# Attention steps of successive chunks put in one group on the TensorE, and value products as column-tiled pairs, in a fused retention and feed-forward kernel

## The chip, the cores and the metric

The kernel runs on one core of a Trainium2 chip. The metric is the device time of an execution in microseconds (us). Executions of a kernel agree within some tenths of a per cent in most cases, with a few one per cent higher; this case is about one to two per cent, so the comparisons below use several rounds on the same chip and, where possible, the trace. A verdict of the timing (faster, same, slower) is drawn at 2%.

## The reference

```python
# q, k, v: [8 batches, 8 heads, 576 tokens, 64]
scores = q @ k.T / sqrt(64)
ret    = scores * gamma[h] ** (i - j)      # for j <= i, else 0
attn   = ret @ v                           # [8, 8, 576, 64]
x      = attn, heads side by side          # [4608 tokens, 512]
h      = x @ w_in                          # [4608, 2048]
g      = h * sigmoid(beta * h)
out    = g @ w_out                         # [4608, 512]
```

## The kernel before

Each batch is cut into chunks of 128, 128, 128, 128 and 64 tokens ("short chunk"), 40 chunks in all. The decay is separable, so it is put into q and v, and what the earlier chunks of a batch contribute is held in a 64x64 state per head. PE is TensorE, ACT is ScalarE, DVE is VectorE and POOL is GpSimd. A row tile is a part of PE's array that takes 64 of its 128 rows, a column tile one that takes 64 of its 128 columns; in the traces here two matmuls on two such tiles start 3 to 4 ns apart. How the array is divided, whole or in tiles, is called the tiling mode here. A chunk has these steps:

- `pre` (POOL): scale and cast q, k and v;
- `a_T` (PE): transpose q and k; ACT copies the result;
- `a_sc` (PE): scores of the chunk with itself, contraction over 64, so head pairs run as row tiles; DVE applies the causal mask, giving R;
- `a_st` (PE): add k^T v to the state in PSUM; ACT copies its diagonal blocks to `sbd`;
- `a_O` (PE): the output product O = state product (`sbd` times q) plus value product (v times R); DVE casts it to `xT`.

The value product is the part that the change is about. Two heads share the 128 output partitions. Before, each head's 64 value columns lay in a 128-column buffer whose other half was zero, so a full-width matmul added zeros to the other head:

```python
vpads = [consts.tile([P, H, P], BF16, name=f"vpad{i}") for i in range(NV)]   # cleared once
...
def a_O(i):
    ...
    n = 0
    if c > 0:
        for p in range(HP):                                   # state product
            nc.tensor.matmul(O[:, p, :cL], sbds[(i - 1) % NS][:, p, :], L["qT"][:, p, :cL],
                             start=(n == 0), stop=False, skip_group_check=True)
            n += 1
    for j in range(2):
        for p in range(HP):                                   # value product, padded
            nc.tensor.matmul(O[:, p, :cL], vp[:cL, 2 * p + j, :], R[:cL, j, p, :cL],
                             start=(n == 0), stop=(j == 1), skip_group_check=True)
            n += 1
    nc.vector.tensor_copy(xT[:, :, n0:n0 + cL], O[:, :, :cL])
```

The feed-forward part runs over blocks of 512 tokens: 16 calls of `up` (4 matmuls of 512 columns each) and 16 of `down` (4 each). The steps of the chunks that the next block needs are strewn among these calls, in three places per chunk (`at` is a place in the list of calls, `F` puts off a call until its place is reached):

```python
def attn_steps(i, at, gap=2.0):
    return [(at - 4, F(pre, i)), (at - 3.9, F(load_next, i)), (at, F(a_T, i)), (at + gap, F(a_sc, i)),
            (at + 2 * gap, F(a_st, i)), (at + 2 * gap, F(a_O, i))]
```

Of the kernel before, what the change touches and what calls it, by code (L numbers as in the profile page):

```python
# [12 lines left out]
BF16 = mybir.dt.bfloat16  # L13
ACT = mybir.ActivationFunctionType
ALU = mybir.AluOpType
# [4 lines left out]
def kernel(  # L20
# [10 lines left out]
    nc = tc.nc  # L31
    B, H, S, D = q.shape
# [3 lines left out]
    P = 128  # L36
    HP = H // 2
    KO = d_model // P
    FO = d_ff // P
    MB = 512  # L40
    NMB = N // MB
# [4 lines left out]
    consts = ctx.enter_context(tc.tile_pool(name="consts", bufs=1))  # L46
# [3 lines left out]
    sb = ctx.enter_context(tc.tile_pool(name="sb", bufs=2))  # L50
# [16 lines left out]
    order = [(b, c) for b in range(B) for c in range(NC)]  # L67
# [15 lines left out]
    for h in range(H):  # L83
# [11 lines left out]
    nc.gpsimd.affine_select(out=causal[:], in_=causal[:], pattern=[[1, P]], compare_op=ALU.is_ge,  # L95
                            fill=0.0, base=0, channel_multiplier=-1)

    NV = 3
    vpads = [consts.tile([P, H, P], BF16, name=f"vpad{i}") for i in range(NV)]

    NS = 2
    sbds = [consts.tile([P, HP, P], BF16, name=f"sbd{i}") for i in range(NS)]
    nc.gpsimd.memset(vpads[0][:], 0.0)
    nc.vector.memset(sbds[0][:], 0.0)
    nc.gpsimd.memset(vpads[1][:], 0.0)
    nc.vector.memset(sbds[1][:], 0.0)


# [57 lines left out]
    live = {}  # L166

    def pre(i):

        b, c = order[i]  # L170
        c0, cL = chunks[c]
        t = qkv_tiles.pop((b, c))
        first = i < 4
        qn = sb.tile([P, H, D], BF16, name="qn", tag="qn", bufs=3)
        kn = sb.tile([P, H, D], BF16, name="kn", tag="kn", bufs=3)
        vp = vpads[i % NV]

        vp4 = vp.rearrange("p (pr two) (x d) -> p pr (two x) d", two=2, x=2)[:, :, 0::3, :]
        gq_b = gq[:cL, c, :].unsqueeze(2).to_broadcast([cL, H, D])
        gv_b = gv[:cL, c, :].unsqueeze(2).to_broadcast([cL, H, D])  # L180
        (nc.vector if first else nc.gpsimd).tensor_tensor(qn[:cL], t[:cL, 0], gq_b, ALU.mult)  # L181
        if first:
            nc.scalar.copy(kn[:cL], t[:cL, 1])
        else:
            nc.gpsimd.tensor_copy(kn[:cL], t[:cL, 1])  # L185
        nc.gpsimd.tensor_tensor(vp4[:cL], t[:cL, 2].rearrange("p (pr two) d -> p pr two d", two=2),  # L186
                                gv_b.rearrange("p (pr two) d -> p pr two d", two=2), ALU.mult)
        live[i] = dict(qn=qn, kn=kn, vp=vp, vp4=vp4)

    def load_next(i):  # L190
        if i + NQ < len(order):
# [2 lines left out]
    def a_T(i):  # L194
        b, c = order[i]
        c0, cL = chunks[c]
        L = live[i]
        T = psum.tile([P, 2, HP, P], BF16, name="T", tag="T", bufs=1)
        for j, src in enumerate((L["qn"], L["kn"])):
            for p in range(HP):  # L200
                nc.tensor.transpose(T[:, j, p, :cL],  # L201
                                    src[:cL, 2 * p:2 * p + 2, :].rearrange("p h d -> p (h d)"),
                                    ident[:cL, :cL])
        qkT = sb.tile([P, 2, HP, P], BF16, name="qkT", tag="qkT", bufs=3)
        nc.scalar.copy(qkT[:, :, :, :cL], T[:, :, :, :cL])  # L205
        L["qT"], L["kT"] = qkT[:, 0], qkT[:, 1]

# [16 lines left out]
    def a_O(i):  # L224
        b, c = order[i]
        c0, cL = chunks[c]
        L = live[i]
        R, vp = L["R"], L["vp"]
        O = psum.tile([P, HP, P], F32, name="O", tag="O", bufs=1)
        n = 0  # L230
        if c > 0:
            for p in range(HP):
                nc.tensor.matmul(O[:, p, :cL], sbds[(i - 1) % NS][:, p, :], L["qT"][:, p, :cL],  # L233
                                 start=(n == 0), stop=False, skip_group_check=True)
                n += 1
        for j in range(2):
            for p in range(HP):
                nc.tensor.matmul(O[:, p, :cL], vp[:cL, 2 * p + j, :], R[:cL, j, p, :cL],  # L238
                                 start=(n == 0), stop=(j == 1), skip_group_check=True)
                n += 1  # L240
        n0 = b * S + c0
        nc.vector.tensor_copy(xT[:, :, n0:n0 + cL], O[:, :, :cL])  # L242
        del live[i]

    def a_st(i):
        b, c = order[i]
        c0, cL = chunks[c]
        L = live[i]
        if c == NC - 1:
            return  # L250
        if c == 0:
            state_ps[b] = psum.tile([P, HP, P], F32, name="st", tag="st", bufs=1)
        st = state_ps[b]
        for p in range(HP):
            nc.tensor.matmul(st[:, p, :], L["kn"][:cL, 2 * p:2 * p + 2, :].rearrange("p h d -> p (h d)"),  # L255
                             L["vp4"][:cL, p], start=(c == 0 and p == 0), stop=True,
                             skip_group_check=True)
        sbd = sbds[i % NS]
        for j in range(2):
            r = slice(j * D, (j + 1) * D)  # L260
            nc.scalar.copy(sbd[r, :, j * D:(j + 1) * D], st[r, :, j * D:(j + 1) * D])  # L261
# [34 lines left out]
    def merged(fill, *streams):  # L296

        todo = sorted((x for st in streams for x in st), key=lambda x: x[0])
        for n, f in enumerate(fill):
            while todo and todo[0][0] <= n:  # L300
                todo.pop(0)[1]()
            f()
        for _, step in todo:
            step()

    def F(f, *a):
        return lambda: f(*a)
# [6 lines that stand above are left out]
    warm_up(12)  # L314
    betas()
    pre(0)
    a_T(0)
    nc.gpsimd.memset(vpads[2][:], 0.0)
    pre(1)
    for i in range(4):  # L320
        warm_up(2)
        a_sc(i)
        a_st(i)
        if i < 3:
            a_T(i + 1)
            if i < 2:
                pre(i + 2)
        else:
            cast_w_in(0)
            warm_up(2)  # L330
        a_O(i)

    fill = [F(up, 0, fo) for fo in range(FO)]
    merged(fill, [(2, F(cast_w_in, 1)), (5, F(cast_w_in, 2)), (9, F(cast_w_in, 3))],
           [(5.1 + g / 10, F(load_w_out, g)) for g in range(2)],
           [(9.1 + g / 10, F(load_w_out, g)) for g in range(2, WG)],
           [(9.5, F(pre, 4)), (12, F(a_T, 4)), (14, F(a_sc, 4)), (16, F(a_O, 4))],
           [(9.6, F(pre, 5)), (15, F(a_T, 5)), (16.1, F(a_sc, 5))], [(9.7, F(pre, 6))])
    for i in range(5):
        load_next(i)  # L340

    q1 = S + chunks[0][1] - MB
    a_st(5)
    a_O(5)
    load_next(5)
    load_next(6)
    fill = [F(up, 1, fo, 0, q1) for fo in range(FO)]
    fill += [F(down, 0, ms, f0) for f0 in range(0, FO, 4) for ms in range(3)]
    fill += [F(down, 0, 3, f0) for f0 in range(0, FO, 4)]
    n1 = len(fill)  # L350
    fill += [F(up, 1, fo, q1, MB - q1) for fo in range(FO)]
    fill += [F(down, 1, ms, f0) for ms in range(MB // P) for f0 in range(0, FO, 4)]
    streams = [[(4, F(cast_w_out, 0)), (10, F(cast_w_out, 1)), (18, F(cast_w_out, 2)), (21, F(cast_w_out, 3))],
               [(0, F(a_T, 6)), (4, F(a_sc, 6)), (8, F(a_st, 6)), (8, F(a_O, 6))],
               attn_steps(7, 23), attn_steps(8, 27)]
    done = 9
    need = lambda m: min(len(order), next((i + 1 for i, (b, c) in enumerate(order)
                                          if b * S + chunks[c][0] + chunks[c][1] >= (m + 1) * MB), len(order)))
    todo = list(range(done, need(2)))
    streams += [attn_steps(i, n1 + n * 30 / len(todo)) for n, i in enumerate(todo)]  # L360
    done = need(2)
    for m in range(2, NMB):
        base = len(fill)
        fill += [F(up, m, fo) for fo in range(FO)]
        fill += [F(down, m, ms, f0) for ms in range(MB // P) for f0 in range(0, FO, 4)]
        if m + 1 < NMB:
            todo = list(range(done, need(m + 1)))
            streams += [attn_steps(i, base + n * 31 / len(todo)) for n, i in enumerate(todo)]
            done = need(m + 1)
    merged(fill, *streams)  # L370


# [28 lines left out]
```

## Time and profile before

| | before |
|---|---|
| time, median | 338.75 us (338.43 to 338.87, 3 runs) |
| span of the profiled execution | 337.1 us |
| PE busy | 325.6 us, 97% |
| ACT, DVE, POOL busy | 48%, 34%, 34% |
| a block of 512 tokens, start to start | 35.86 and 34.08 us, in turn |
| the projections of the last block, which has no attention, by starts | 27.63 us |

These are the busy times and the chain of work that ended last, from the page of the kernel before (PEld is PE's loading of weights, SPq and POOLq are sequencers that issue work, "issue" is time in which nothing is seen to be waited for).

```profile
PE 325.6 (97%) x2455; PEld 174.0 (52%) x2455; DVE 114.0 (34%) x202; ACT 163.1 (48%) x272; POOL 115.0 (34%) x132
PE 84%; DMA 7%; SPq 4%; issue 1%; DVE 1%; ACT 1%; POOL 0%; POOLq 0%
```

PE is nearly always busy and the chain runs on it. That alone does not say how much a cheaper PE step saves, since the ends of matmuls are modelled. The starts are what to read. The next lines are the PE timeline of the kernel before over one full chunk (start in us, duration in us, engine, line, operation, tile rows and columns, moving operand, count).

```profile
193.43 0.39 PE L201 MATMUL T<-ident,qn 128*128 128x128 bf16 x4
193.65 0.39 PE L201 MATMUL T<-ident,kn 128*128 128x128 bf16 x4
193.87 1.89 PE L285 MATMUL po<-w_out_sb,gT 128*128 128x512 bf16 x8
195.70 0.40 PE L217 MATMUL sc<-qkT 64*128 64x128 bf16 x8
196.03 1.90 PE L285 MATMUL po<-w_out_sb,gT 128*128 128x512 bf16 x8
197.76 0.39 PE L255 MATMUL st<-vpad,kn 128*128 128x128 bf16 x4
197.99 0.39 PE L233 MATMUL O<-qkT,sbd 128*128 128x128 bf16 x4
198.21 0.61 PE L238 MATMUL O<-R,vpad 128*128 128x128 bf16 x8
198.66 0.60 PE L285 MATMUL po<-w_out_sb,gT 128*128 128x512 bf16 x2
```

Differences of starts give the price of each step. The value product (L238) takes 198.66 - 198.21 = 0.45 us: 8 matmuls of 128 columns, 56 ns each. State and state product take 0.22 us each. Eight matmuls of 512 columns take 8 x 0.216 = 1.73 us, yet from 193.87 to the scores at 195.70 there are 1.83 us: 0.10 us are lost as the PE goes from whole-array matmuls (128\*128) to row tiles (64\*128). On the way back the loss repeats: the eight scores run as four pairs, 56 ns apart, 0.22 us in all, but the next projection starts 0.33 us after the scores began. It then goes on 12 ns late. So a change of tiling mode costs about 0.105 us, and about half of the scores' 0.44 us is changes. Transposes, state, state product and value product fit between projections without a gap.

The cost of a full chunk is thus 0.45 + 0.44 + 0.22 + 0.22 + 0.45 = 1.78 us. By the counts in the trace the longer of the two kinds of block runs the steps of five chunks, four full ones and a short one, as a batch has them; the shorter kind has one full chunk less, and 35.86 - 34.08 = 1.78 us again. So the five chunks of a batch cost 35.86 - 27.63 = 8.23 us, 1.65 us for an average chunk. The lengths of their steps in the trace add up to the same 8.23.

### The profile page before, as it was taken

What the parts mean: (1) busy time and instruction counts of PE and PEld (TensorE: products, weight loads), DVE (VectorE), ACT (ScalarE), POOL (GpSimd) and SP (SyncE); (2) the same over time, 40 slices, a digit from 0 to 9 for tenths busy, and PEclk for the clock granted to TensorE, in tenths of its full rate; (3) what the DMA queues carried; (4) which work ended last, traced back from release to release, by engine and by line L of the source; (5) the groups of instructions that cost most, each with busy time, mean ns of one, the idle gap of its engine ahead of it and who ended that gap; (6) DMA issues with size and microseconds to landing.
All of it is one profiled execution on the core that took longest, in us unless ns stands there. A gap on an engine that the chain in (4) does not pass through costs nothing.

```text
span 337.1 us, 6009 instructions
## 1 busy us (share of the span) xinstructions
PE 325.6 (97%) x2455; PEld 174.0 (52%) x2455; DVE 114.0 (34%) x202; ACT 163.1 (48%) x272; POOL 115.0 (34%) x132
## 2 busy tenths in 40 slices
PE   5979899999999999999999999999999999999995
PEld 2644574676554555545555555545555555544442
DVE  4664373623321244213332432223224432320011
ACT  2767671385246623752376227712782257404800
POOL 5224767875324433323334432233333330000000
PEclk9799999999999999999999999999999999999999
DMA  9999999999999737906492549036400100011011
GB/s 173 222 387 212 243 377 214 199 212 229 234 222 246 146 111 172 172 0 158 116 228 48 117 118 214 9 87 159 114 2 31 61 36 0 14 55 57 2 61 63
DMA packets 121979, 46.53 MB, mean 138 GB/s; under 512 B 113232, under 2 KB 113248, under 8 KB 121952
## 3 DMA queue, kind: packets, MB, share of 16 engines
q1 hardware_dynamic: 121920, 46.15, 61.3%
q8 instruction: 19, 0.31, 0.4%
q14 instruction: 8, 0.07, 0.1%
q10 hardware_dynamic: 32, 0.01, 0.0%
HBM read 36.71 MB, written 9.44 MB: 137 GB/s over the span
## 4 chain that ended last, share of the span: by engine, by line
PE 84%; DMA 7%; SPq 4%; issue 1%; DVE 1%; ACT 1%; POOL 0%; POOLq 0%
PE po L285 38%; PE ph L273 32%; DMA qkvn<-in_q_dram 4%; PE O L238 4%; PE T L201 4%; SPq L63 4%; PE sc L217 3%; DMA wt<-in_moe_w_out_dram 2%; PE st L255 2%; PE O L233 2%; SPq L122 1%; ACT gT L275 1%; DVE w_out_sb L141 0%; DVE R L221 0%; ACT qkT L205 0%
## 5 line engine op out<-in xcount | busy, mean ns | idle before, releaser
L273 PE MATMUL ph<-xT,w_in_sb 128*128 128x512 bf16 (+2 forms) x640 | 134.2, 358 | 1.7 <-DVE xT L242 1.7
L285 PE MATMUL po<-w_out_sb,gT 128*128 128x512 bf16 x576 | 133.6, 380 | 0.0
L275 ACT ACTIVATE gT<-ph,beta_sb 128x512 bf16<-128x512 f32 (+2 forms) x160 | 102.0, 645 | 41.2 <-PE ph L273 39.9
L273 PEld LDWEIGHTS <-w_in_sb 128*128 128x128 bf16 x640 | 58.4, 98 | 55.5 <-issue 1.6
L285 PEld LDWEIGHTS <-gT 128*128 128x128 bf16 x576 | 53.3, 98 | 57.9
L221 DVE TENSOR_TENSOR R<-sc,causal 128x512 bf16<-128x512 f32 (+1 forms) x80 | 47.2, 631 | 101.1 <-PE sc L217 101.0
L205 ACT COPY qkT<-T 128x1024 bf16<-128x1024 bf16 (+1 forms) x40 | 36.9, 924 | 68.6 <-PE T L201 68.5
L181 POOL TENSOR_TENSOR qn<-qkvn,gq 128x512 bf16<-128x512 f32 (+1 forms) x36 | 37.9, 1052 | 49.9 <-PE T L201 46.4
L186 POOL TENSOR_TENSOR vpad<-qkvn,gv 128x512 bf16<-128x512 f32 (+1 forms) x40 | 41.6, 1041 | 28.2 <-PE O L238 14.9
L291 DVE COPY ot<-po 128x512 f32<-128x512 f32 x36 | 24.8, 691 | 67.5 <-PE po L285 65.1
L185 POOL CAST kn<-qkvn 128x512 bf16<-128x512 f32 (+1 forms) x36 | 21.9, 608 | 69.5 <-issue 65.7
L261 ACT CAST sbd<-st 64x256 bf16<-64x256 f32 x64 | 23.3, 364 | 43.4 <-PE st L255 42.6
L242 DVE CAST xT<-O 128x512 bf16<-128x512 f32 (+1 forms) x40 | 25.5, 637 | 38.0 <-PE O L238 38.0
L238 PE MATMUL O<-R,vpad 128*128 128x128 bf16 (+1 forms) x320 | 23.7, 214 | 1.4 <-DVE R L221 1.2
L238 PEld LDWEIGHTS <-vpad 128*128 128x128 bf16 (+1 forms) x320 | 18.2, 97 | 2.8 <-issue 2.2
L217 PEld LDWEIGHTS <-qkT 64*128 64x128 bf16 (+1 forms) x320 | 8.9, 98 | 17.3 <-ACT qkT L205 7.1
L201 PE MATMUL T<-ident,qn 128*128 128x128 bf16 (+1 forms) x160 | 15.1, 218 | 2.5 <-DVE qn L181 2.4
L201 PEld LDWEIGHTS <-qn 128*128 128x128 bf16 (+1 forms) x160 | 11.1, 99 | 11.9 <-DVE qn L181 2.4
L217 PE MATMUL sc<-qkT 64*128 64x128 bf16 (+1 forms) x320 | 15.5, 217 | 0.6 <-ACT qkT L205 0.4
L201 PE MATMUL T<-ident,kn 128*128 128x128 bf16 (+1 forms) x160 | 14.9, 216 | 0.3 <-POOL kn L185 0.3
L255 PEld LDWEIGHTS <-kn 128*128 128x128 bf16 x128 | 9.5, 99 | 6.6 <-issue 0.2
L255 PE MATMUL st<-vpad,kn 128*128 128x128 bf16 x128 | 12.7, 222 | 0.0
(40 smaller groups left out, 80.0 us busy)
## 6 DMA issues: line engine op xcount, KB each, us to landing
out_dram<-ot SPq DMA_DIRECT2D x36, 256.0 KB, 2.2
qkvn<-in_q_dram SPq DMA_DIRECT2D x32, 256.0 KB, 4.8
qkvn<-in_k_dram SPq DMA_DIRECT2D x32, 256.0 KB, 5.1
qkvn<-in_v_dram SPq DMA_DIRECT2D x32, 256.0 KB, 5.0
wt<-in_moe_w_in_dram SPq DMA_DIRECT2D x4, 1024.0 KB, 10.6
wt<-in_moe_w_out_dram SPq DMA_DIRECT2D x4, 1024.0 KB, 10.2
qkvn<-in_q_dram SPq DMA_DIRECT2D x8, 128.0 KB, 4.0
qkvn<-in_k_dram SPq DMA_DIRECT2D x8, 128.0 KB, 3.6
```

Of the source, the lines that this page charges most:

```text
L181: (nc.vector if first else nc.gpsimd).tensor_tensor(qn[:cL], t[:cL, 0], gq_b, ALU.mult)
L186: nc.gpsimd.tensor_tensor(vp4[:cL], t[:cL, 2].rearrange("p (pr two) d -> p pr two d", two=2), gv_b.rearrange("p (pr two) d -> p pr two d", ...
L201: nc.tensor.transpose(T[:, j, p, :cL], src[:cL, 2 * p:2 * p + 2, :].rearrange("p h d -> p (h d)"), ident[:cL, :cL])
L205: nc.scalar.copy(qkT[:, :, :, :cL], T[:, :, :, :cL])
L217: nc.tensor.matmul(sc[j][:cL, p, :cL], L["kT"][r, p, :cL], L["qT"][r, p, :cL], start=True, stop=True, skip_group_check=True)
L221: nc.vector.tensor_tensor(R[:cL, j, :, :cL], sc[j][:cL, :, :cL], m_b, ALU.mult)
L238: nc.tensor.matmul(O[:, p, :cL], vp[:cL, 2 * p + j, :], R[:cL, j, p, :cL], start=(n == 0), stop=(j == 1), skip_group_check=True)
L242: nc.vector.tensor_copy(xT[:, :, n0:n0 + cL], O[:, :, :cL])
L255: nc.tensor.matmul(st[:, p, :], L["kn"][:cL, 2 * p:2 * p + 2, :].rearrange("p h d -> p (h d)"), L["vp4"][:cL, p], start=(c == 0 and p == 0 ...
L273: nc.tensor.matmul(ph[:, :tn], w_in_sb[:, ko, fo * P:(fo + 1) * P], xT[:, ko, x0:x0 + tn], start=(ko == 0), stop=(ko == KO - 1))
L275: nc.scalar.activation(gT[:, fo, t0:t0 + tn], ph[:, :tn], ACT.Silu, scale=beta_sb[:, fo:fo + 1])
L285: nc.tensor.matmul(po[:], gT[:, fo, ms * P:(ms + 1) * P], w_out_sb[:, fo, :], start=(fo == 0), stop=(fo == FO - 1))
```

## The change

Its intent is to halve the value product: the two heads of a pair become two column tiles of 64 columns that run at once, without padding. As this gives the value product a tiling mode of its own, the steps of three successive chunks (transposes of chunk i, scores of i-1, output and state of i-2) are put into one group, so that the modes follow on one another. From chunk 9 on there is one group per chunk; chunks 0 to 8 keep their places. The diff, cut to its core:

```diff
-        vp = vpads[i % NV]
-        nc.gpsimd.tensor_tensor(vp4[:cL], ...)                 # strided, into padded buffers
+        vn = sb.tile([P, H, D], BF16, name="vn", tag="vn", bufs=4)
+        nc.gpsimd.tensor_tensor(vn[:cL], t[:cL, 2], gv_b, ALU.mult)
...
         O = psum.tile([P, HP, P], F32, name="O", tag="O", bufs=1)
+        for p in range(HP):
+            for j in range(2):
+                nc.tensor.matmul(O[j * D:(j + 1) * D, p, :cL], vn[:cL, 2 * p + j, :], R[:cL, j, p, :cL],
+                                 start=(p == 0), stop=(c == 0), skip_group_check=True)
         if c > 0:
             for p in range(HP):
                 nc.tensor.matmul(O[:, p, :cL], sbds[(i - 1) % NS][:, p, :], L["qT"][:, p, :cL],
-                                 start=(n == 0), stop=False, skip_group_check=True)
-                n += 1
-        for j in range(2):
-            for p in range(HP):
-                nc.tensor.matmul(O[:, p, :cL], vp[:cL, 2 * p + j, :], R[:cL, j, p, :cL], ...)
+                                 start=False, stop=True, skip_group_check=True)
...
+    def cluster(i, at):
+        last = len(order) - 1
+        st = []
+        if i <= last:
+            st += [(at - 4, F(pre, i)), (at - 3.9, F(load_next, i)), (at, F(a_T, i))]
+        if C0 <= i - 1 <= last:
+            st += [(at, F(a_sc, i - 1))]
+        if C0 <= i - 2 <= last:
+            st += [(at, F(a_O, i - 2)), (at, F(a_st, i - 2))]
+        return st
...
+        todo = list(range(done, need(m + 1) + 2))
+        streams += [cluster(i, base + n * 31 / len(todo)) for n, i in enumerate(todo)]
```

Left out: one more buffer each for k and for the transposed q and k, the state's matmuls, which now read `vn`, and the clearing of the padded buffers, which falls away.

More of the change, by code (lines that the diff above doesn't have):

```diff
@@ L96 @@
                             fill=0.0, base=0, channel_multiplier=-1)
-    NV = 3
-    vpads = [consts.tile([P, H, P], BF16, name=f"vpad{i}") for i in range(NV)]
     NS = 2
     sbds = [consts.tile([P, HP, P], BF16, name=f"sbd{i}") for i in range(NS)]
-    nc.gpsimd.memset(vpads[0][:], 0.0)
     nc.vector.memset(sbds[0][:], 0.0)
-    nc.gpsimd.memset(vpads[1][:], 0.0)
     nc.vector.memset(sbds[1][:], 0.0)
@@ L174, in pre @@
         qn = sb.tile([P, H, D], BF16, name="qn", tag="qn", bufs=3)
-        kn = sb.tile([P, H, D], BF16, name="kn", tag="kn", bufs=3)
-        vp = vpads[i % NV]
-        vp4 = vp.rearrange("p (pr two) (x d) -> p pr (two x) d", two=2, x=2)[:, :, 0::3, :]
+        kn = sb.tile([P, H, D], BF16, name="kn", tag="kn", bufs=4)
+        vn = sb.tile([P, H, D], BF16, name="vn", tag="vn", bufs=4)
         gq_b = gq[:cL, c, :].unsqueeze(2).to_broadcast([cL, H, D])
@@ L185, in pre @@
             nc.gpsimd.tensor_copy(kn[:cL], t[:cL, 1])
-        nc.gpsimd.tensor_tensor(vp4[:cL], t[:cL, 2].rearrange("p (pr two) d -> p pr two d", two=2),
-                                gv_b.rearrange("p (pr two) d -> p pr two d", two=2), ALU.mult)
-        live[i] = dict(qn=qn, kn=kn, vp=vp, vp4=vp4)
+        nc.gpsimd.tensor_tensor(vn[:cL], t[:cL, 2], gv_b, ALU.mult)
+        live[i] = dict(qn=qn, kn=kn, vn=vn)
     def load_next(i):
@@ L203, in a_T @@
                                     ident[:cL, :cL])
-        qkT = sb.tile([P, 2, HP, P], BF16, name="qkT", tag="qkT", bufs=3)
+        qkT = sb.tile([P, 2, HP, P], BF16, name="qkT", tag="qkT", bufs=4)
         nc.scalar.copy(qkT[:, :, :, :cL], T[:, :, :, :cL])
@@ L227, in a_O @@
         L = live[i]
-        R, vp = L["R"], L["vp"]
+        R, vn = L["R"], L["vn"]
         O = psum.tile([P, HP, P], F32, name="O", tag="O", bufs=1)
-        n = 0
+        for p in range(HP):
+            for j in range(2):
+                nc.tensor.matmul(O[j * D:(j + 1) * D, p, :cL], vn[:cL, 2 * p + j, :], R[:cL, j, p, :cL],
+                                 start=(p == 0), stop=(c == 0), skip_group_check=True)
         if c > 0:
@@ L233, in a_O @@
                 nc.tensor.matmul(O[:, p, :cL], sbds[(i - 1) % NS][:, p, :], L["qT"][:, p, :cL],
-                                 start=(n == 0), stop=False, skip_group_check=True)
-                n += 1
-        for j in range(2):
-            for p in range(HP):
-                nc.tensor.matmul(O[:, p, :cL], vp[:cL, 2 * p + j, :], R[:cL, j, p, :cL],
-                                 start=(n == 0), stop=(j == 1), skip_group_check=True)
-                n += 1
+                                 start=False, stop=True, skip_group_check=True)
         n0 = b * S + c0
         nc.vector.tensor_copy(xT[:, :, n0:n0 + cL], O[:, :, :cL])
-        del live[i]
     def a_st(i):
@@ L255, in a_st @@
             nc.tensor.matmul(st[:, p, :], L["kn"][:cL, 2 * p:2 * p + 2, :].rearrange("p h d -> p (h d)"),
-                             L["vp4"][:cL, p], start=(c == 0 and p == 0), stop=True,
+                             L["vn"][:cL, 2 * p:2 * p + 2, :].rearrange("p h d -> p (h d)"), start=(c == 0 and p == 0), stop=True,
                              skip_group_check=True)
@@ L317 @@
     a_T(0)
-    nc.gpsimd.memset(vpads[2][:], 0.0)
     pre(1)
@@ L358 @@
                                           if b * S + chunks[c][0] + chunks[c][1] >= (m + 1) * MB), len(order)))
-    todo = list(range(done, need(2)))
-    streams += [attn_steps(i, n1 + n * 30 / len(todo)) for n, i in enumerate(todo)]
-    done = need(2)
-    for m in range(2, NMB):
-        base = len(fill)
+    C0 = done
+    clusters = []
+    def cluster(i, at):
[8 more added lines that the diff above has]
+        return st
+    for m in range(1, NMB - 1):
+        base = n1 if m == 1 else len(fill)
+        if m > 1:
+            fill += [F(up, m, fo) for fo in range(FO)]
+            fill += [F(down, m, ms, f0) for ms in range(MB // P) for f0 in range(0, FO, 4)]
+        todo = list(range(done, need(m + 1) + 2))
+        streams += [cluster(i, base + n * 31 / len(todo)) for n, i in enumerate(todo)]
+        done = need(m + 1) + 2
+    for m in range(NMB - 1, NMB):
         fill += [F(up, m, fo) for fo in range(FO)]
         fill += [F(down, m, ms, f0) for ms in range(MB // P) for f0 in range(0, FO, 4)]
-        if m + 1 < NMB:
-            todo = list(range(done, need(m + 1)))
-            streams += [attn_steps(i, base + n * 31 / len(todo)) for n, i in enumerate(todo)]
-            done = need(m + 1)
     merged(fill, *streams)
```

## The prediction

> **What bounds it now.** TensorE: the page has PE busy 97%, and the chain of waits runs on PE for 84% of the span, almost unbroken from 46 to 333 us; before that it is loading. In the timeline, 512-column matmuls start every 216 ns: the projections, 1,152 of them, are 249 us. ACT (48%), DVE and POOL (34% each) have slack; from chunk 15 on, loads land 8 us or more before use. A block of 512 tokens takes 34.1 or 35.8 us, mean 34.95; its projections are 27.65 (the last block, without attention, takes that). So attention costs 7.3 us per 4.5 chunks, 1.62 us per chunk, all on the critical path.
>
> **A full chunk's PE time** (timeline, start to start): transposes 8 x 55.5 ns = 0.44 us; scores 0.43; state 0.22; state product 0.22; value product 8 x 55.5 = 0.44. The scores already run in row-tiled pairs, 4 ns apart, a pair each 56 ns: 0.22 of streaming and 0.21 of two mode changes (the next start comes 311 instead of 216 ns later on entry, 147 instead of 56 on exit, and the matmul after it 12 late). A change thus costs about 0.105 us; this agrees with the Trainium skill, "TensorEngine Tiling (Array Packing)", Key Properties, that changing the mode drains the array.
>
> **What the change does.**
> 1. Value products become column-tiled pairs: 4 x 56 ns instead of 8 x 55.5, -0.22 us per full chunk, if the halves run together. The same page says (Restrictions) that column tiling disables Fast Weight Load. The short chunk's 64x64 scores load 64-column weights and still start a pair each 28 ns, so I estimate two loads at 56 ns, just hidden.
> 2. That product needs its own mode. Alone, it adds two changes (0.21) and gains nothing: chunks 0 to 8, in their old places, gain about zero. In a group (transposes, scores, values, state product, state) there are three changes instead of two: +0.105. Hence the grouping.
> 3. The short chunk's transposes share the mode of the next scores, and its value product shares an exit: about -0.3 us per batch.
> Over the five kinds of group, five chunks cost 7.3 us instead of 8.1: -0.16 us per chunk, x 31 grouped chunks = -4.8 us.
> 4. The halves are interleaved and need the second masked score at once, so a value product that waits for DVE (near 45.9 us) ends later: +0.3 us.
> 5. Off the path, 0: POOL's three clearings of 0.95 us and strided writes; two more chunks in block 1, whose loads land by 80 us, before their transposes; ACT's 1.0 + 0.75 us of copies at once per group, which three PSUM buffers cover.
>
> **Prediction:** 338.75 - 4.5 = 334.3 us, range 331.0 to 338.5. Faster by over 2%: 0.13; within 2%: 0.83; slower: 0.04.
>
> **What would show it.** Value products starting in pairs a few ns apart, a pair each 56 to 60 ns; gaps of about 95 ns at three mode changes per group; blocks of about 34.2 us on average; first projection near 22 us and last block of 27.65 unchanged; no new PE waits for DVE, ACT or loads.
>
> **What would make it wrong.** If the weight loads of two column tiles are not hidden behind matmuls, a pair takes 80 to 110 ns or more, and the gain shrinks to nothing or a loss of 1%. If passing from row-tiled to column-tiled costs less drain, up to 3 us more are gained. If the group blocks ACT so long that projections wait for PSUM, blocks grow in the first projection.

## The result, and the profile after

The changed kernel took 333.5 us (median of 4 runs, 333.25 to 335.33) against 338.59 us (median of 4, the three above and one more). The ratio was 0.9861 with a 95% interval of 0.9825 to 0.9897. A ratio here is the mean time of one kernel's runs over that of the other's of the same rounds, so not quite the ratio of the medians. Executions over 1.5% slower than the fastest of the same kernel are left out of the means. In a later job with 6 runs it had 333.69 us and 0.9851 (0.9820 to 0.9882). The interval says that 1.0 to 1.8% were gained.

The page of the changed kernel, busy times and chain:

```profile
PE 318.0 (96%) x2415; PEld 169.1 (51%) x2455; DVE 111.3 (34%) x202; ACT 165.5 (50%) x272; POOL 110.3 (33%) x129
PE 94%; DVE 3%; issue 1%; ACT 0%
```

The second line ought to be read with care: the chain now goes through PE at the start too, where before it went through loads, but a second trace of the same changed kernel (the run "again" below) has PE 85%, DMA 7% and SPq 5%, so this differs from execution to execution and is not what the change did. The first line shows a trap as well: 2,415 matmuls are recorded where there are 2,455, so 40 records are missing, and the PE's busy time must not be compared with the 325.6 of before. Starts stay good. The PE timeline of the changed kernel over one group with full chunks:

```profile
191.68 0.39 PE L193 MATMUL T<-ident,qn 128*128 128x128 bf16 x4
191.90 0.39 PE L193 MATMUL T<-ident,kn 128*128 128x128 bf16 x4
192.22 0.40 PE L209 MATMUL sc<-qkT 64*128 64x128 bf16 x8
192.55 0.41 PE L224 MATMUL O<-R,vn 128*64 128x128 bf16 x8
192.90 0.40 PE L228 MATMUL O<-qkT,sbd 128*128 128x128 bf16 x4
193.13 0.39 PE L243 MATMUL st<-vn,kn 128*128 128x128 bf16 x4
193.57 0.59 PE L273 MATMUL po<-w_out_sb,gT 128*128 128x512 bf16 x2
```

The first projection after this group is one of those missing records: L243 started at 193.13 and takes 0.22, so the projections go on at 193.355 and the line at 193.57 is the second. The group takes 193.355 - 191.68 = 1.675 us where the three places of before took 1.78. The value product from its start to the next step is 0.35 us, of which 0.10 is the change of mode; one change to the scores and one to the values precede it.

How the value products (with their loads of weights) look among the groups of instructions, before and after, columns: busy us and mean ns of one, then idle time before them:

```profile
L238 PE MATMUL O<-R,vpad 128*128 128x128 bf16 x256 | 20.5, 219 | 1.4 <-DVE R L221 1.2
L238 PEld LDWEIGHTS <-vpad 128*128 128x128 bf16 x256 | 15.9, 98 | 2.4 <-issue 2.2
```

```profile
L224 PE MATMUL O<-R,vn 128*64 128x128 bf16 x256 | 14.4, 227 | 2.0 <-DVE R L213 2.0
L224 PEld LDWEIGHTS <-vn 128*64 128x64 bf16 x256 | 9.0, 110 | 5.8 <-issue 3.0
```

A narrow load is recorded longer than a wide one (110 against 98 ns), although it has half the columns, but it is hidden: in the trace the pairs start 3 ns apart, and the pairs follow one another after 80, 56 and 56 ns. Only the first interval after the change of mode is long, by 24 ns; for the scores it is 11 ns.

By stages: the two stand almost equal at 46 us (the batch of first projections there starts at 46.12 us before and 46.16 after, and block 1 begins at 66.77 and 66.62); the blocks in the middle take 35.03 and 33.45 to 33.58 us, from one first `up` to the next, instead of 35.86 and 34.08; the last block is the same. The last block starts at 300.15 us instead of 305.50, and this 5.35 us is the whole gain of the profiled execution (337.1 to 331.7).

### The profile page after: what moved, and what is told of

The parts are those of the page before. It is cut to its first block, busy times and chain, and to the rows that moved or that the text cites. A ratio compares the mean times of both kernels' runs of the same rounds, so it can differ in the third digit from the quotient of the medians.

```text
span 331.7 us, 5914 instructions
## 1 busy us (share of the span) xinstructions
PE 318.0 (96%) x2415; PEld 169.1 (51%) x2455; DVE 111.3 (34%) x202; ACT 165.5 (50%) x272; POOL 110.3 (33%) x129
## 4 chain that ended last, share of the span: by engine, by line
PE 94%; DVE 3%; issue 1%; ACT 0%
PE ph L261 38%; PE po L273 37%; PE T L193 5%; PE O L224 4%; PE sc L209 4%; PE O L228 3%; PE st L243 2%; PE ph L146 2%; DVE R L213 2%; DVE xT L231 0%; ACT qkT L197 0%; DVE w_in_sb L124 0%; DVE tiny L153 0%; DVE ot L279 0%; DVE qn L174 0%
## 5 line engine op out<-in xcount | busy, mean ns | idle before, releaser
L261 PE MATMUL ph<-xT,w_in_sb 128*128 128x512 bf16 (+2 forms) x622 | 126.9, 357 | 2.2 <-DVE xT L231 1.1
L273 PE MATMUL po<-w_out_sb,gT 128*128 128x512 bf16 x556 | 125.7, 379 | 1.1
L261 PEld LDWEIGHTS <-w_in_sb 128*128 128x128 bf16 x640 | 60.5, 98 | 60.0 <-issue 1.6
L273 PEld LDWEIGHTS <-gT 128*128 128x128 bf16 x576 | 55.3, 98 | 63.2
L179 POOL TENSOR_TENSOR vn<-qkvn,gv 128x512 bf16<-128x512 f32 (+1 forms) x40 | 41.6, 1040 | 65.9 <-PE st L243 26.7
L224 PE MATMUL O<-R,vn 128*64 128x128 bf16 (+1 forms) x320 | 16.9, 221 | 2.0 <-DVE R L213 2.0
L224 PEld LDWEIGHTS <-vn 128*64 128x64 bf16 (+1 forms) x320 | 10.6, 109 | 7.3 <-issue 3.9
L243 PE MATMUL st<-vn,kn 128*128 128x128 bf16 x128 | 12.7, 223 | 0.0
L228 PE MATMUL O<-qkT,sbd 128*128 128x128 bf16 (+1 forms) x128 | 11.9, 215 | 0.0
```

Of the source, the lines that this page charges most:

```text
L179: nc.gpsimd.tensor_tensor(vn[:cL], t[:cL, 2], gv_b, ALU.mult)
L224: nc.tensor.matmul(O[j * D:(j + 1) * D, p, :cL], vn[:cL, 2 * p + j, :], R[:cL, j, p, :cL], start=(p == 0), stop=(c == 0), skip_group_check ...
L261: nc.tensor.matmul(ph[:, :tn], w_in_sb[:, ko, fo * P:(fo + 1) * P], xT[:, ko, x0:x0 + tn], start=(ko == 0), stop=(ko == KO - 1))
L273: nc.tensor.matmul(po[:], gT[:, fo, ms * P:(ms + 1) * P], w_out_sb[:, fo, :], start=(fo == 0), stop=(fo == FO - 1))
```

## The experiments

The theory is a balance: paired value products save 0.22 us per full chunk, each change of tiling mode costs 0.105 us, and the grouping is there to save changes. Its rivals: that the pairs are the whole gain and the grouping only tidiness; that fewer interruptions of the projections are the gain; or that narrow products are cheaper in themselves. All runs gave correct results unless said otherwise. To turn a ratio into us, it is taken times 338.6 here.

### Pairs in their old places

The changed kernel with the schedule of before (cut):

```diff
-    for m in range(1, NMB - 1): ... cluster(i, base + n * 31 / len(todo)) ...
+    streams += [attn_steps(i, n1 + n * 30 / len(todo)) for n, i in enumerate(todo)]
+    ... # as in the kernel before
```

> Value products as column-tiled pairs, but every step of a chunk in the place that it had before (transposes, scores and values in three separate places). Theory (two mode changes of 0.105 us each eat the 0.22 us that the pairs save): 338.6 us, within 0.8 us of the kernel before; the value block of a full chunk takes as long as before, about 0.45 us with its changes. Rival (the pairs are the whole gain, the grouping is only tidiness): 333.5 us, as the changed kernel.

Measured: 338.1 us, ratio 0.9955 (0.9929 to 0.9981), so 1.5 us below the kernel before, with 0.6 to 2.4 as the interval. The kernel before was spread wide in this job (338.19 to 340.63). The profile fell into an execution at about half the TensorE clock (549.55 us; the granted clock, the share of the full clock that was let through, was 0.559), and no length can be read from it. So it was run again:

> The pairs in their old places once more, because the profile of their first run fell at a clock of 0.56 and its lengths say nothing. From the changed kernel's trace a full value block then costs 0.22 us of pairs, 0.025 of a slower first pair and 0.21 of two changes: 0.46 against 0.45 us before; the short chunk's about 0.1 us less than before. So 338 us, 0.3 to 1.0 us below the kernel before; a full block clearly under 0.45 us would speak for a cheaper change.

Measured: 338.58 us, ratio 0.9994 (0.9953 to 1.0035). The PE timeline of this run, state, values and state product of a full chunk between projections:

```profile
195.51 1.90 PE L273 MATMUL po<-w_out_sb,gT 128*128 128x512 bf16 x8
197.25 0.39 PE L243 MATMUL st<-vn,kn 128*128 128x128 bf16 x4
197.56 0.41 PE L224 MATMUL O<-R,vn 128*64 128x128 bf16 x8
197.91 0.40 PE L228 MATMUL O<-qkT,sbd 128*128 128x128 bf16 x4
```

The state's four matmuls end their turn at 197.25 + 0.22 = 197.47, and the state product starts at 197.91: 0.44 us for values with two changes of mode, as long as the padded ones took. The blocks take 35.78 and 34.00 us, 0.08 less than before each, which fits the short chunk. The two timings together leave something between nothing and 1.5 us; the trace says 0.8 (336.3 against 337.1). The first rival falls: without the grouping the pairs give a small part of the gain, by the traces 0.8 of 5.3 us. This run also has the added buffers and POOL's smaller work, so these are not the gain either.

### Groups with padded values

The kernel before with the schedule of the changed one, its added buffers for k and the transposed q and k, and a fourth padded buffer (cut):

```diff
-    NV = 3
+    NV = 4
-    streams += [attn_steps(i, base + n * 31 / len(todo)) ...]
+    streams += [cluster(i, base + n * 31 / len(todo)) ...]
```

> Groups as in the changed kernel, but value products full width with padded values, 8 x 56 ns (four padded buffers, so that the groups do not wait for one). Theory: a group has two mode changes instead of three, the short chunk's steps share modes with their neighbours; from the lengths in the traces 7.77 us per five chunks against 8.23 before and 7.41 changed, so -0.09 us x 31 = -2.9 us: 335.7 us. Rival A (fewer interruptions of the projections are the gain): 333.5 us. Rival B (grouping alone gives nothing): 338.6 us.

Measured: 337.55 us, ratio 0.9944 (0.9914 to 0.9973), 1.9 us below the kernel before. The 2.9 us expected are just at the end of the interval, but the trace gives less and shows the slip: the expectation let the short chunk's value product follow the scores in one mode, but in the code of before the state product stands between them. That group takes 1.43 us, not 1.23, and the five kinds of group sum to 8.02 us instead of the 7.77 expected; against 8.23 before this gives -0.21 / 5 x 31 = -1.3 us, within the interval. Rival A would have had to give all 5 us. Grouping alone is worth about a quarter to two fifths of the gain; in the trace all of it comes from one place, the short chunk's transposes, which share the mode of the next scores (that group takes 1.56 us with its entry, where the same steps took 1.77 apart). Four lines of that group in the PE timeline of this run, its first and last among them:

```profile
166.43 0.29 PE L201 MATMUL T<-ident,qn 64*128 64x64 bf16 x4
166.66 0.40 PE L217 MATMUL sc<-qkT 64*128 64x128 bf16 x7
166.99 0.40 PE L233 MATMUL O<-qkT,sbd 128*128 128x128 bf16 x4
167.89 0.81 PE L272 MATMUL ph<-xT,w_in_sb 128*128 128x512 bf16 x3
```

From 166.43 to 167.89 there are 1.46 us, and the entry costs 0.10.

### Value products not alternating between the tiles

```diff
-        for p in range(HP):
-            for j in range(2):
+        for j in range(2):
+            for p in range(HP):
                 nc.tensor.matmul(O[j * D:(j + 1) * D, p, :cL], ...)
```

> The changed kernel, but all four value products of the first column tile are issued before the four of the second, so that neighbours in the queue share a tile and can't run together. Theory (the saving is that two tiles stream at once): seven or eight intervals of 56 ns per full chunk instead of four, +0.17 to +0.22 us per grouped chunk: 338 to 340 us. Rival (narrow weights are cheaper in themselves, or the queue overlaps the tiles whatever the order): 333.5 us.

Measured: 334.4 us, ratio 0.9852 (0.9824 to 0.9880), the same as the changed kernel's 0.9851 (which is from another job, on another chip; each ratio is to the kernel before in its own job). The theory as it was written down here fell: the order of issue hardly matters (a block of 35.03 us takes 35.08). The PE timeline of this run:

```profile
192.64 0.40 PE L209 MATMUL sc<-qkT 64*128 64x128 bf16 x8
192.97 0.42 PE L224 MATMUL O<-R,vn 128*64 128x128 bf16 x8
193.33 0.40 PE L228 MATMUL O<-qkT,sbd 128*128 128x128 bf16 x4
```

The eight value products take 0.36 us, as with alternation. One by one they start at 192.971, .984, 193.051, .064, .107, .120, .163 and .176: pairs again, 13 ns apart instead of 3. The compiled program has all four of the first tile ahead of the four of the second. So matmuls of the second tile started before earlier ones of the first. The changed kernel's own trace shows the same with names, in a group whose transposes (rows 0 to 63 only) are followed by scores in the same mode:

```profile
199.62 0.22 PE L193 MATMUL T<-ident,kn 64*128 64x64 bf16 x2
199.66 0.23 PE L209 MATMUL sc<-qkT 64*128 64x128 bf16 x1
199.68 0.22 PE L193 MATMUL T<-ident,kn 64*128 64x64 bf16 x2
199.72 0.40 PE L209 MATMUL sc<-qkT 64*128 64x128 bf16 x7
```

In the program all eight transposes come before the scores; a score started between them, presumably one of the row tile that the transposes leave free. The Trainium skill says otherwise, in "TensorE: Matmul & The Clock Gate", Part 3, The mechanism: "MATMULs are pc-monotone in start AND end". The starts in these traces are not; the ends are modelled and say nothing.

This left a gap: if order does not matter, is it overlap or are narrow products cheap? The next experiment but one was made for that.

### The state product between scores and values

Lines in brackets stand for code that is cut:

```diff
-        (value products, then state product)
+        if c > 0:
+            for p in range(HP):
+                nc.tensor.matmul(O[:, p, :cL], sbds[(i - 1) % NS][:, p, :], ..., start=(p == 0), stop=False, ...)
+        (value products, start=(c == 0 and p == 0), stop=True)
```

> The changed kernel with the state product (128x128 mode) put between the scores (64x128) and the value products (128x64): the same matmuls, one mode change more in each of the 25 groups that have a state product. Theory (a change costs about 0.105 us whatever the two modes): +2.6 us, 336.1 us. Rival (passing between two tiled modes costs about as much as two changes, so the detour is free, or drains are hidden): 333.5 us.

Measured: 336.61 us, ratio 0.9925 (0.9889 to 0.9960). The changed kernel on another chip had 0.9851, the nearly equal kernel of the section above 0.9852 in the same job: 0.0073 x 338.6 = 2.5 us for the same matmuls with 25 changes more, 0.10 us each. The PE timeline of a full group:

```profile
193.38 0.39 PE L193 MATMUL T<-ident,qn 128*128 128x128 bf16 x4
193.61 0.39 PE L193 MATMUL T<-ident,kn 128*128 128x128 bf16 x4
193.93 0.40 PE L209 MATMUL sc<-qkT 64*128 64x128 bf16 x8
194.26 0.40 PE L224 MATMUL O<-qkT,sbd 128*128 128x128 bf16 x4
194.59 0.41 PE L228 MATMUL O<-R,vn 128*64 128x128 bf16 x8
194.93 0.40 PE L243 MATMUL st<-vn,kn 128*128 128x128 bf16 x4
195.16 0.38 PE L273 MATMUL po<-w_out_sb,gT 128*128 128x512 bf16 x1
```

It takes 195.16 - 193.38 = 1.78 us instead of 1.675: from one tiled mode to the other directly costs one change, not two, and a detour costs one more.

### Both heads on one column tile

```diff
+                jt = j if c == 0 else 0
-                nc.tensor.matmul(O[j * D:(j + 1) * D, p, :cL], vn[:cL, 2 * p + j, :], ...
+                nc.tensor.matmul(O[jt * D:(jt + 1) * D, p, :cL], vn[:cL, 2 * p + j, :], ...
```

Cut: the value products' own `start` is adapted, and the state product then starts the accumulation anew, so that nothing unwritten is read. The result is wrong (relative error 0.5).

> The changed kernel with both heads' value products sent to the same column tile for all chunks but the first of a batch: same count, same narrow weights, same modes, but no second tile to run in. The result is wrong on purpose. Theory (the saving is that two tiles stream at once, in whatever order they are issued): eight starts 56 ns apart, +0.22 us in 18 full and +0.12 us in 7 short grouped chunks, +4.8 us: 338.3 us. Rival (narrow products are cheaper by themselves): 333.5 us.

Measured: 339.35 us, ratio 1.0009 (0.9978 to 1.0040). Against the changed kernel of the same job that is 0.0158 x 338.6 = 5.3 us, and the kernel is back where it was before the change. The PE timeline:

```profile
195.51 0.40 PE L209 MATMUL sc<-qkT 64*128 64x128 bf16 x8
195.84 0.63 PE L225 MATMUL O<-R,vn 128*64 128x128 bf16 x8
196.41 0.40 PE L229 MATMUL O<-qkT,sbd 128*128 128x128 bf16 x4
```

The value products take 0.57 us instead of 0.35; single starts are 80 and then 56 ns apart. Same count, same widths, same modes, one tile: the saving is gone. The rival "narrow is cheaper" falls, and the overlap of two tiles is shown to be the saving. The half microsecond beyond the expected 4.8 fits the chunks 6 to 8, which come after loading ends and had been left out of the sum (3 x 0.22 us).

### The changed kernel again

> The changed kernel itself once more, to have it on the same chip as the three runs beside it: 333.5 us, ratio to the kernel before 0.986.

Measured: 333.69 us, ratio 0.9851 (0.9820 to 0.9882).

### State updates as column-tiled pairs too: a better kernel

If a change of mode is the price and a matmul in an open mode is cheap, more should be put into the open mode. The state update computes a 128x128 product per head pair, of which only the two 64x64 blocks on the diagonal are used. As column tiles it streams 64 columns instead of 128, and it can follow the value products without a change:

```diff
     def a_O(i, between=None):
         ... value products ...
+        if between is not None:
+            between()                       # state update of this chunk
         ... state product ...
+    def st_mm(i):
+        ...
+            for p in range(HP):
+                for j in range(2):
+                    nc.tensor.matmul(st[j * D:(j + 1) * D, p, j * D:(j + 1) * D], L["kn"][:cL, 2 * p + j, :],
+                                     L["vn"][:cL, 2 * p + j, :], start=(c == 0 and p == 0), stop=True, ...)
```

> An attempt at a better kernel. In the groups of batches 2 to 7 the state update also runs in column-tiled pairs, right after the value products and so in their mode: only the two diagonal 64x64 blocks of each head pair, 4 pairs of 64 columns, 29 ns each, instead of 4 x 56 ns of 128 columns; no mode change more. Theory: -0.106 us in each of 24 groups, -2.5 us: 331.0 us. Rival (loads of 64-column weights are the limit of a column-tiled pair, 56 ns whatever the stream): no gain, 333.5 us.

Measured: 331.48 us (331.21 to 332.93), ratio 0.9777 (0.9749 to 0.9806), correct. Against the changed kernel of the same job it is 0.0074 x 338.6 = 2.5 us less, as expected, and against the kernel before it gains 1.9 to 2.5%; as the interval reaches past 0.98, the verdict by the 2% rule is unclear. The PE timeline:

```profile
190.50 0.39 PE L193 MATMUL T<-ident,qn 128*128 128x128 bf16 x4
190.73 0.39 PE L193 MATMUL T<-ident,kn 128*128 128x128 bf16 x4
191.04 0.40 PE L209 MATMUL sc<-qkT 64*128 64x128 bf16 x8
191.37 0.41 PE L224 MATMUL O<-R,vn 128*64 128x128 bf16 x8
191.62 0.29 PE L247 MATMUL st<-vn,kn 128*64 128x64 bf16 x8
191.84 0.40 PE L230 MATMUL O<-qkT,sbd 128*128 128x128 bf16 x4
```

The state update starts 0.25 us after the values, with no gap, and its four pairs follow one another in 29 to 32 ns; so the weight loads are hidden even at that pace, and the rival falls.

### The balance of all of them

The lengths of the five kinds of group (by the starts in the trace, with the late entry of those whose first step changes the mode) add up to the cost of five chunks. The longer kind of block less 27.63 us gives the same within 0.01; the rows of the pairs in old places, of the order of issue and of the one tile are from that block alone. Times 31 grouped chunks, this gives each kernel's time from its trace alone:

| kernel | five chunks, us | (difference to before) / 5 x 31 | timed, by ratio |
|---|---|---|---|
| before | 8.23 | | |
| pairs in old places | 8.15 | -0.5 | -1.5 and -0.2 |
| groups, padded values | 8.02 | -1.3 | -1.9 |
| both heads on one tile | 8.19 | -0.2 | +0.3 |
| state product between | 7.82 | -2.5 | -2.5 |
| values not alternating | 7.45 | -4.8 | -5.0 |
| changed | 7.41 | -5.1 | -5.0 |
| state updates tiled too | 7.00 | -7.6 | -7.5 |

Per five chunks the pairs alone save 0.08 us and the groups alone 0.21, but both together 0.82: each half pays because of the other.

## Why the prediction was right

The prediction of 334.3 us was right: 333.5 us was measured, well inside its range, and the mechanism is the one it named.

- **The bound.** It held. The groups' PE time fell by 5.1 us by the sums above, and the span of the profiled execution by 5.3.
- **Step 1, pairs at 56 ns.** The pairs start 3 ns apart and 56 ns after one another, as said; the first interval after entering is 80. That overlap is the saving is shown by sending both heads to one tile, which cost 5.3 us. The estimate that two weight loads need 56 ns, "just hidden", set no limit: when the state updates were tiled too, pairs with loads just as narrow followed one another in 29 to 32 ns.
- **Step 2, a mode of its own gains nothing alone.** Shown by the pairs in their old places: 0.44 us per value product, with changes, against 0.45.
- **Step 3, the short chunk.** The padded groups gained 1.3 us by their trace, 0.21 us per five chunks, all from the transposes that share a mode; of the 0.3 us per batch the part of the value product was not measured alone.
- **The sum.** It said 7.3 us instead of 8.1 per five chunks; the traces have 7.41 and 8.23. Both were low by 0.1. The 8.1 came from the mean of the two kinds of block, whose nine chunks have two short ones, while the five of a batch have one and so cost more. The 7.3 left out that the first interval of the column-tiled pairs is long by 24 ns and not by 11, which is 0.07 us in five groups; the rest was not worked out. That the errors cancelled, 0.166 us per chunk against 0.16, was luck.
- **Step 4, +0.3 us near 45.9 us.** The delay is there, in the size that was predicted, but it did not reach the end. After DVE's mask (R) PE had half of the padded value products left to do; now it has the paired ones and the state product, and DVE's cast of O waits 0.80 us instead of 0.47. The DVE timeline before and after:

```profile
44.57 1.27 DVE L221 TENSOR_TENSOR R<-sc,causal 128x512 bf16<-128x512 f32 x2
46.32 0.69 DVE L242 CAST xT<-O 128x512 bf16<-128x512 f32 x1 [0.47 <-PE O L238]
```

```profile
44.28 1.27 DVE L213 TENSOR_TENSOR R<-sc,causal 128x512 bf16<-128x512 f32 x2
46.36 0.69 DVE L231 CAST xT<-O 128x512 bf16<-128x512 f32 x1 [0.80 <-PE O L228]
```

The next projections start only 0.04 us later because the mask began 0.29 us earlier. It began at 44.28 to 44.51 us in the seven full-clock traces with pairs, and at 44.57 and 44.96 in the two with padded values; why was not tested. The same 0.33 us delays the first projection, which the prediction had said would not move: it starts at 22.61 us in the second trace of the changed kernel, against 22.28 before. In the first trace it is 23.28, since one small DVE step took 0.84 instead of 0.17 us and the first transposes came at 9.14 instead of 8.39 us. Such a step of 0.7 to 1.0 us is in seven of the nine full-clock traces, the padded groups' too, and not in the second one of the changed kernel, so it is not the change; why it comes was not tested. The late first projection does not show further on: with 22.61 us block 1 begins at 66.65, with 23.28 at 66.62. Without this term the prediction would have been 334.0.
- **Step 5, things off the path.** No block grew in its projections: those in the middle are 0.5 to 0.8 us shorter each, which is what their groups save. Block 1 takes 30.94 instead of 29.12 us, because two more chunks' steps are in it, and the last block with attention is shorter for the same reason (30.47 instead of 33.86).

## What to carry to other kernels

Read the price of a step from the differences of starts, with the gaps where the PE changes its tiling mode; here a change cost 0.105 us, half of what the paired value products of a full chunk saved, so tiling a short run of matmuls paid only when runs of different chunks were put side by side and shared changes. Once a mode is open, see what else fits into it: the state update, at half its columns, gave another 2.5 us for no change more. Issue order between tiles needed no care here, but two products on one tile do not overlap.

## What the Trainium skill lacked or had wrong

- "TensorE: Matmul & The Clock Gate", Part 3, The mechanism: it has matmuls strictly in program order of start. Here matmuls of one tile start before earlier ones of another: eight value products issued four and four started in pairs 13 ns apart, and a score started at 199.66 us before two transposes, from 199.68 on, that precede it in the program.
- "TensorEngine Tiling (Array Packing)", Key Properties: it says that changing the mode drains the array, and the late starts in the traces fit that; it has no figure. Here a change cost about 0.105 us (a start 92 to 99 ns late and the following one 10 to 12), from whole array to row tiles, row to column tiles and back alike; only on entering the column tiles was the following one 24 ns late.
- The same page, Restrictions: it says that column tiling disables Fast Weight Load. Loads were recorded at 110 instead of 98 ns, which may be that, but they cost no time: pairs of 64-column products still followed each other in 29 to 32 ns.
- "TensorE: Matmul & The Clock Gate", Part 1: it describes half rate as the idle state, which some microseconds of activity release, and warns that the gate was seen stuck low for 50 us and more. In one of the six executions of the pairs in their old places the granted clock stayed at half for nearly the whole of 548 us, although PE was 98% busy, and the time was 549.55 us instead of 338.1. Nothing here shows why.
